# Crossbar DMA transposes and casting weight loads in an attention and MLP kernel

## The chip, the cores and the metric

The kernel runs on one core of one Trainium2 chip. The metric is the device time of one execution in microseconds (us). A profile is one execution recorded by the hardware profiler; its span, from the first to the last instruction, is about 2 us shorter than the timed run.

Engine names: PE is TensorE (matmuls and transposes), PEld its weight loads, DVE is VectorE, ACT is ScalarE, POOL is GpSimd, SP is SyncE, which only issues DMAs here. A name with q at the end (SPq) is that engine's sequencer or its DMA queue.

## The reference

Two parts in sequence: an attention with exponential feature maps, and a normalised two-layer MLP with a residual.

```python
# q, k, v: (8, 8, 576, 64); w_phi: (64, 128); w_ch1: (512, 2048); w_ch2: (2048, 512)
def phi(x):
    proj = x @ w_phi
    proj = proj - max(abs(proj), axis=-1)
    return concat([exp(proj), exp(-proj)], axis=-1)
q_p, k_p = phi(q), phi(k)
kv  = einsum('bhsf,bhsd->bhfd', k_p, v);   z = sum(k_p, axis=2)
num = einsum('bhsf,bhfd->bhsd', q_p, kv);  den = einsum('bhsf,bhf->bhs', q_p, z) + 1e-6
x   = heads_to_columns(num / den)                      # (8, 576, 512)
xn  = (x - mean(x)) / sqrt(var(x) + 1e-6) * g_ln
out = x + relu(xn @ w_ch1) @ w_ch2
```

## The kernel before

The batch is worked in four pairs of two. A pair has eight attention units, then a normalised x of nine tiles of 128 tokens, then the MLP on these. A list scheduler in the program fixes the order of the instructions on every engine beforehand: each operation is added with an estimate of its time, a rank, the keys that it reads and writes, and the engines that may do it. So all engines run in a fixed order, and an operation that waits holds up all that stand behind it on its engine. The MLP of one pair is interleaved with the attention of the next.

In the profile `qkT_ps` and `qkT` are transposed q and k, `pm` and `pt` their feature products, `kv` and `num` the attention products, `xc` the centred tokens, `xT` their transposes, `hT` the first MLP product (768 matmuls) and `ch` the second.

Every transpose is a TensorE matmul against an identity. It writes to PSUM, the memory of TensorE's results, and VectorE or ScalarE then copies (evicts) it to SBUF, where the operands of the next matmul lie:

```python
def a_trans(u, V):                       # q and k of one unit
    def products(i):
        qkb = qk_bufs[g % NBUF].bitcast(BF16)
        # ... PSUM tile qkT_ps ...
        for c in range(4):
            nc.tensor.transpose(
                u["qkT_ps"][:, (i * 4 + c) * P : (i * 4 + c + 1) * P],
                qkb[:, i, u["uu"], 4 * c * D + 1 : 4 * (c + 1) * D : 2], ident)
    def copy(e, i):
        # ...
        copy_on(e, u["qkT"][:, i * 512 : (i + 1) * 512], u["qkT_ps"][:, i * 512 : (i + 1) * 512])
    # ... i = 1 for k, 0 for q; the copies on DVE or ACT
```

```python
def center():                            # always on VectorE
    # ... r = t // NM, and the tile xc
    nc.vector.tensor_scalar(out=pr["xc", r][:, t % NM, :], in0=x[:, t, :],
                            scalar1=pr["mv"][:, t, 0:1], scalar2=None, op0=ALU.subtract)
# x_trans: 3 transposes of xc into a PSUM tile for each of 4 column blocks, then copies to xT
```

The weights come as fp32 into staging (the x buffers of later pairs), and are cast to bf16 by ScalarE or GpSimd; w1 is multiplied by g on the way:

```python
def load_w1(n, queue, rank):             # issued from SP
    dma(queue, rank, 1 << 20, stage(n), moe_w_ch1[...], w=[("stage", n % 2)])
def cast_w1(n, rank):
    # for each kc: w1_sb[...] = stage(n)[...] * gln_sb[:, kc]   on ACT or POOL
def cast_w2(n, rank):
    # for each block: w2_sb[...] = stage(n)[...]                on ACT or POOL
```

## Time and profile before

| | before |
|---|---|
| median of 2 runs | 419.39 us (418.72 to 420.06) |
| span of the profile | 417.9 us |
| TensorE busy | 371.7 us, 89% |
| first hT product | 66.7 us |

The first part of the page of the kernel before gives busy time, share of the span and number of instructions of each engine:

```profile
PE 371.7 (89%) x3575; PEld 229.1 (55%) x3632; DVE 274.7 (66%) x705; ACT 268.1 (64%) x569; POOL 171.7 (41%) x336
```

Averages hide that there are two stages. The windows view of the kernel before has, for each stretch: its length, busy us of each engine (with the number of instructions), the granted TensorE clock, the busy share of the 16 DMA engines and GB/s:

```profile
core 0: us, PE busy (x) PEld busy (x) DVE busy (x) ACT busy (x) POOL busy (x), PEclk, DMA share, GB/s
...
20.00:60.00 40.00, 26.29 (x339) 19.55 (x344) 32.17 (x93) 33.06 (x69) 37.06 (x68) 0.79 1.10 271
60.00:100.00 40.00, 30.59 (x316) 19.97 (x319) 31.42 (x85) 29.41 (x68) 23.68 (x47) 0.91 0.65 186
100.00:140.00 40.00, 39.20 (x411) 24.34 (x416) 27.21 (x67) 25.43 (x55) 14.86 (x32) 1.00 0.37 113
```

From 100 us on TensorE is full at full clock. From 20 to 60 us it is starved, at a clock of 0.79, while GpSimd is busy 37.1 of 40 us. The chain of waits of the kernel before (start, length, what) shows GpSimd as the engine that was waited for in that stretch:

```profile
52.04 1.55 POOL w L359
53.60 0.51 POOL x L718 x2
54.10 1.00 POOL vv L605
...
60.02 3.08 POOL w L359 x2
```

`w L359` is the cast and scaling of w1. What the transposes cost TensorE is read from the timeline of the kernel before (start, length, engine, line, operation), by the distance between starts, because the ends of pipelined matmuls overlap:

```profile
111.46 0.39 PE L513 MATMUL qkT_ps<-ident,qk 128*128 128x128 bf16 x4
111.69 0.81 PE L945 MATMUL ch_ps<-w,hT 128*128 128x512 bf16 x3
112.33 0.39 PE L513 MATMUL qkT_ps<-ident,qk 128*128 128x128 bf16 x4
112.56 0.81 PE L915 MATMUL hT_ps<-xT,w 128*128 128x384 bf16 x4
```

Four transposes hold TensorE for 0.22 to 0.23 us, 55 to 57 ns each. The mean durations in the next view are longer, about 220 to 240 ns, and must not be used as a cost. In the groups view of the kernel before (line, engine, operation, number; busy us and mean ns; idle time before, with releasers) these are the groups that the change touches:

```profile
L513 PE MATMUL qkT_ps<-ident,qk 128*128 128x128 bf16 x256 | 27.5, 241 | 6.0 <-DMA qk<-in_k_dram 5.0 <-DMA qk<-in_q_dram 0.7
L870 PE MATMUL xT_ps<-ident,xc 128*128 128x128 bf16 x144 | 14.3, 219 | 1.0 <-DVE xc L841 0.3 <-DVE hT L923 0.3 <-DVE numc L706 0.2
L359 POOL TENSOR_SCALAR w<-x,gln 128x512 bf16<-128x512 f32 x10 | 15.5, 1563 | 1.3 <-DMA x<-in_moe_w_ch_dram 1.3
L841 DVE TENSOR_SCALAR xc<-x,mv 128x512 bf16<-128x512 bf16 x36 | 14.1, 409 | 0.0
```

### The profile page before, as it was taken

What the parts mean: (1) busy time and instruction counts of PE and PEld (TensorE: products, weight loads), DVE (VectorE), ACT (ScalarE), POOL (GpSimd) and SP (SyncE); (2) the same over time, 40 slices, a digit from 0 to 9 for tenths busy, and PEclk for the clock granted to TensorE, in tenths of its full rate; (3) what the DMA queues carried; (4) which work ended last, traced back from release to release, by engine and by line L of the source; (5) the groups of instructions that cost most, each with busy time, mean ns of one, the idle gap of its engine ahead of it and who ended that gap; (6) DMA issues with size and microseconds to landing.
All of it is one profiled execution on the core that took longest, in us unless ns stands there. A gap on an engine that the chain in (4) does not pass through costs nothing.

```text
span 417.9 us, 9371 instructions
## 1 busy us (share of the span) xinstructions
PE 371.7 (89%) x3575; PEld 229.1 (55%) x3632; DVE 274.7 (66%) x705; ACT 268.1 (64%) x569; POOL 171.7 (41%) x336
## 2 busy tenths in 40 slices
PE   3657756888999899989999999889999999999995
PEld 2545534555556565656666655566565655555542
DVE  3768976987676779897567878966676778110111
ACT  4978884877585766876666757785667725533320
POOL 4799896553444453153243534344444420000000
PEclk9986797999999999999999999999999999999999
DMA  7999999742314641414242423300100001001003
GB/s 198 339 249 261 289 301 258 216 142 78 108 49 135 171 148 50 127 53 127 77 127 76 127 77 121 109 2 5 49 27 27 27 34 54 16 27 50 27 25 100
DMA packets 48956, 46.81 MB, mean 112 GB/s; under 512 B 15504, under 2 KB 40208, under 8 KB 48912
## 3 DMA queue, kind: packets, MB, share of 16 engines
q1 hardware_dynamic: 47680, 45.62, 37.2%
q10 hardware_dynamic: 1232, 0.59, 0.5%
q8 instruction: 28, 0.46, 0.5%
q14 instruction: 16, 0.13, 0.1%
HBM read 36.77 MB, written 9.44 MB: 111 GB/s over the span
## 4 chain that ended last, share of the span: by engine, by line
PE 69%; DVE 14%; POOL 5%; SPq 4%; ACT 3%; DMA 2%; issue 2%; DVEq 0%; ACTq 0%
PE ch_ps L945 27%; PE hT_ps L915 25%; SPq L275 4%; PE num L694 4%; DVE m L562 4%; PE kv L663 3%; DVE st L834 3%; PE pm L543 3%; PE qkT_ps L513 3%; DVE xc L841 2%; POOL vv L605 2%; PE pt L636 2%; POOL x L718 1%; DMA v<-in_v_dram 1%; DVE numc L700 1%
## 5 line engine op out<-in xcount | busy, mean ns | idle before, releaser
L915 PE MATMUL hT_ps<-xT,w 128*128 128x384 bf16 x768 | 151.9, 327 | 3.6 <-ACT hT L925 1.2
L945 PE MATMUL ch_ps<-w,hT 128*128 128x512 bf16 x536 | 143.8, 379 | 4.3 <-DVE qkT L266 1.6
L925 ACT ACTIVATE hT<-hT_ps 128x384 bf16<-128x384 f32 x140 | 68.1, 491 | 75.0 <-PE hT_ps L915 74.4
L718 POOL TENSOR_TENSOR x<-numc,rden 128x192 bf16<-128x192 f32 (+1 forms) x112 | 50.7, 462 | 120.4 <-DVE rden L712 107.3
L915 PEld LDWEIGHTS <-w 128*128 128x128 bf16 x768 | 71.0, 98 | 53.3 <-issue 4.5
L562 DVE TENSOR_REDUCE m<-pm 128x8 f32<-128x1024 f32 x64 | 76.5, 1209 | 8.1 <-PE pm L543 8.0
L945 PEld LDWEIGHTS <-hT 128*128 128x128 bf16 x576 | 50.9, 98 | 43.1 <-DVE qkT L266 2.1
L642 ACT ACTIVATE ea<-pt 128x1024 bf16<-128x1024 f32 x64 | 63.1, 1032 | 5.2 <-PE num L694 2.7
L591 ACT ACTIVATE EB<-pm 128x1024 bf16<-128x1024 f32 x64 | 63.4, 1023 | 0.6 <-DVE m L562 0.6
L952 DVE SCALAR_TENSOR_TENSOR o<-ch_ps,rstd,x 128x512 f32<-128x512 f32 x36 | 26.5, 743 | 50.6 <-PE ch_ps L945 50.2
L605 POOL TENSOR_TENSOR vv<-v,emk 128x512 bf16<-128x512 f32 x32 | 33.6, 1051 | 54.6 <-issue 29.1
L700 DVE TENSOR_TENSOR numc<-num,emq 128x195 f32<-128x195 f32 (+1 forms) x96 | 33.0, 347 | 29.1 <-PE num L694 21.3
L694 PEld LDWEIGHTS <-ea 128*128 128x128 bf16 x512 | 29.3, 102 | 15.3 <-issue 2.4
L923 DVE TENSOR_SCALAR hT<-hT_ps 128x384 bf16<-128x384 f32 x52 | 28.4, 546 | 12.4 <-PE hT_ps L915 12.0
L694 PE MATMUL num<-KV,ea 128*128 128x65 bf16 x512 | 33.6, 199 | 2.4 <-DVE qkT L266 0.8
L706 DVE TENSOR_TENSOR numc<-numc,num 128x195 f32<-128x195 f32 (+1 forms) x100 | 33.7, 344 | 1.4
L605 POOL TENSOR_TENSOR vv<-v,en 128x512 bf16<-128x512 f32 x32 | 33.4, 1044 | 0.6 <-DVE rden L712 0.3
L513 PE MATMUL qkT_ps<-ident,qk 128*128 128x128 bf16 x256 | 27.5, 241 | 6.0 <-DMA qk<-in_k_dram 5.0
L663 PEld LDWEIGHTS <-EB 128*128 128x128 bf16 x512 | 23.9, 103 | 11.9 <-issue 9.0
L663 PE MATMUL kv<-vv,EB 128*128 128x65 bf16 x512 | 28.2, 201 | 0.0
L513 PEld LDWEIGHTS <-qk 128*128 128x128 bf16 x256 | 20.1, 108 | 14.4 <-DMA qk<-in_k_dram 5.8
L834 DVE BATCH_NORM_STATS2 st<-x 128x6 f32<-128x512 bf16 x36 | 24.5, 680 | 2.7 <-POOL x L718 2.7
(64 smaller groups left out, 410.4 us busy)
## 6 DMA issues: line engine op xcount, KB each, us to landing
x<-in_moe_w_ch_dram SPq DMA_DIRECT2D x8, 1024.0 KB, 8.7
out_dram<-o SPq DMA_DIRECT2D x32, 256.0 KB, 2.3
qk<-in_k_dram SPq DMA_DIRECT2D x28, 256.0 KB, 3.6
v<-in_v_dram SPq DMA_DIRECT2D x28, 256.0 KB, 3.3
qk<-in_q_dram SPq DMA_DIRECT2D x26, 256.0 KB, 4.9
qk<-in_k_dram SPq DMA_DIRECT2D x2, 512.0 KB, 9.3
qk<-in_q_dram SPq DMA_DIRECT2D x2, 512.0 KB, 10.2
v<-in_v_dram SPq DMA_DIRECT2D x2, 512.0 KB, 9.1
```

Source lines behind the costliest of these rows:

```text
L513: nc.tensor.transpose(u["qkT_ps"][:, (i * 4 + c) * P : (i * 4 + c + 1) * P], qkb[:, i, u["uu"], 4 * c * D + 1 : 4 * (c + 1) * D : 2], ident,)
L562: nc.vector.reduce_max(out=u["m", i].rearrange("p (c e) -> p e c", e=2), in_=u["pm", i], axis=AX.X, apply_absolute_value=True,)
L591: nc.scalar.activation(u["EB"][:, t].rearrange("p c f -> p (c f)"), u["pm", 1].rearrange("p e c f -> p (e c f)"), AF.Exp, scale=(1.0, -1.0 ...
L605: nc.gpsimd.tensor_tensor(out=u["vv"][:, t, 0:MX, 0:D], in0=vb[:, uu, :].rearrange("p (c d) -> p c d", d=D), in1=bcast(e[:, 0:MX], 2, D), ...
L642: nc.scalar.activation(u["EA"][:, t, :], u["pt"], AF.Exp, scale=(1.0, -1.0)[t])
L663: nc.tensor.matmul(ps[:, t, c // 4, :], EB[:, t, (c % 2) * 4 + c // 2, :], vv[:, t, c, :], start=False, stop=(t == 0 and c == MX - 1), ski ...
L694: nc.tensor.matmul(ps[:, t, i, :], lhsT, rhs, start=(j == 0), stop=(j == len(terms) - 1))
L700: nc.vector.tensor_tensor(out=st["numc"][:, 0:nch], in0=st["ps"][:, 1], in1=bcast(em_of(), 2, D1), op=ALU.mult,)
L718: nc.gpsimd.tensor_tensor(out=dst, in0=st["numc"][:, i : i + cnt, 0:D], in1=bcast(st["rden"][:, i : i + cnt], 2, D), op=ALU.mult,)
L915: nc.tensor.matmul(st["ps"], w1_sb[:, kc, jj * P : (jj + 1) * P], pr["xT", r][:, kc, :], start=(kc == 0), stop=(kc == KC - 1),)
L925: nc.scalar.activation(h_sb, st["ps"], AF.Relu)
L945: nc.tensor.matmul(ch[t], hT[r, jj][:, rt * P : (rt + 1) * P], w2_sb[:, jj, :], start=(jj == 0), stop=(jj == JC - 1),)
```

## The change

The intent is to take transposes from TensorE and casts from GpSimd. (1) From the second pair on, q and k of a unit are cast to bf16 in one instruction, and one DMA that transposes on its way (`dma_start_transpose`, called a crossbar transpose here) writes `qkT`; `xc` goes to `xT` in the same way. (2) The weights are cast by the DMA that loads them, issued by GpSimd and held back until a `vv` product on GpSimd; g is then multiplied into w1 in place by VectorE or GpSimd. (3) Centring may go to VectorE or GpSimd. Around this the change makes the xT evictions wider and the x keys finer, gives `qkT` three buffers in place of two and x three in place of four, and reorders priorities. Its core:

```diff
+        if u["pair"]:
+            def cast(e):
+                u["qkb"] = att.tile([P, 2, MX * D], BF16, tag="qkb", name="qkb")
+                copy_on(e, u["qkb"], qk_bufs[g % NBUF][:, :, u["uu"], :])
+            def turn():
+                u["qkT"] = att.tile([P, 1024], BF16, tag="qkT", name="qkT", bufs=NQ)
+                nc.sync.dma_start_transpose(
+                    out=u["qkT"].rearrange("p (c n) -> p c n", n=P),
+                    in_=u["qkb"].rearrange("p i f -> p (i f)"))
+            add_any({"POOL": 1.1, "ACT": 0.95, "DVE": 0.6}, V, cast, ...)
+            add("SP", 0.7, V, turn, ...)
+            add("DMA", 1.0, V, None, ...)
+            return
 ...
+            add_any({"DVE": 0.25, "POOL": 0.75}, V, center, ...)        # was DVE alone
 ...
+        if pr["pair"]:
+            for i in range(n):
+                def turn(i=i):
 ...
+                    nc.sync.dma_start_transpose(
+                        out=pr["xT", r][:, :, i * P : (i + 1) * P], in_=pr["xc", r][:, i, :])
 ...
-    def load_w1(n, queue, rank):        # fp32 into stage(n), then cast_w1 on ACT or POOL
+    def load_w1(n, rank, after):
+        dma("POOL", rank, 1200000, w1_sb[:, :, n * WC : (n + 1) * WC], moe_w_ch1[...],
+            r=after, w=[("w1", n, kc) for kc in range(KC)])
+    def scale_w1(n, rank):
+        ...
+                w = w1_sb[:, kc, n * WC : (n + 1) * WC]
+                ENG[e].tensor_scalar_mul(out=w, in0=w, scalar1=gln_sb[:, kc : kc + 1])
+            add_any({"DVE": 0.22, "POOL": 0.62}, rank, emit, ...)
 ...
+                after = [("vv", 0, n % 2)]
```

## The prediction

> **What bounds the kernel now.** Two stages. From 100 to 413 us TensorE is the bound: the windows view has it busy 303.4 of 313 us at clock 1.00, and the waits view gives it no wait above 1.6 us there. Before that it is starved: in 0 to 66.7 us it is busy 40.4 us at a mean clock of 0.83, with DMA share 1.03, ACT 50.9 and GpSimd 55.6. The first hT product stands at 66.7 us, when all 144 kv products of pair 0 are issued. From 28 to 66 us the chain of waits runs again and again through GpSimd (vv, x, and three w1 casts of 1.56 us between 52 and 63 us); TensorE's largest wait there is kv on GpSimd's vv, 8.5 us.
>
> **What the change removes.** In TensorE order, 192 of 256 qkT transposes and 108 of 144 xT transposes. Timeline, steady stage: four transposes hold TensorE 0.22 us start to start, 55 ns each. The Trainium skill ("TensorE: Matmul & The Clock Gate", "Wait — 56ns, not 53.3ns?") says 55.6; the trace agrees. So 300 x 55.6 ns = 16.7 us off the bounding engine, nearly all on the path. Their evictions go too (qkT halves 0.42 us DVE, 0.59 us ACT), and the staged weight casts: 15.5+4.9 us GpSimd, 8.7 us ACT.
>
> **What it adds.** 24 q/k casts, mostly on ACT (about 1 us, estimated from the 1.03 us ACT passes over 128x1024), and 51 crossbar transposes on the SP queue, 9.8 MB, against a DMA share of 0.23. In the start-up: five w1 scalings on GpSimd (1.56 us, if like the casts), eleven on DVE (0.41 us, like centring), eight GpSimd-issued weight DMAs[...]. All 27 later centrings move to GpSimd, probably 1.5 us each against 0.41 on DVE. "VectorE: DVE Perf Modes" (The three transpose paths) gives 1309 ns for one 128x128 crossbar transpose; if eight serialised, 10.5 us would fill a unit's slot (about 11 us). I expect them spread over engines and 3 to 5 us to landing, hidden by three qkT buffers.
>
> **Start-up.** The new TensorE order puts the first hT at kv 108, not 144; 64 hT (10.4 us) stand before kv 144. With GpSimd freed of casts I expect the first hT near 57 us and the steady stage about 10 us earlier.
>
> **Give-back.** At each of the three pair boundaries stats, GpSimd centring and crossbar are a longer chain than before; before, TensorE lost 3.1 us at 260-280. I allow 4-5 us in all.
>
> **Sum.** 419.4 - 16.7 - 10 + 4 = about 397 us. I say 396, 8 in 10 from 382 to 409. Faster by over 2%: 0.93; within 2%: 0.06; slower: 0.01.
>
> **What would show it.** 64 qkT and 36 centred transposes left on TensorE; first hT at 55-60 us; no TensorE wait on qkT's crossbar DMA above 2 us; short TensorE holes at the pair boundaries; a higher DMA share; GpSimd busy about 40 us up by centring, 20 down by casts.
>
> **What would make it wrong.** Crossbar transposes slow or serialised (over 8 us landing), so that TensorE waits for qkT or xT; SP's in-order queue holding loads or stores behind a transpose that waits for its cast; casting DMAs taking several us of GpSimd each, or taking start-up bandwidth so that q/k/v land late; GpSimd centring opening holes of 5 us or more per pair. Or, downward, a much shorter start-up (385 or less).

## More of the kernel before

Part 3 of the page of the kernel before gives packets, megabytes and the share of the 16 DMA engines' time for each queue:

```profile
q1 hardware_dynamic: 47680, 45.62, 37.2%
```

## The result

The changed kernel took 398.84 us (398.57 to 399.10, two runs), against 419.39 before: a ratio of 0.951, with an interval of 0.9439 to 0.9581. A ratio here is the mean time of one kernel's fast runs over that of the other's of the same rounds, so not quite the ratio of the medians. The later sets have their own runs of the kernel before, with medians of 419.66 to 420.44 us. Differences in us from the changed kernel are taken below between medians, against 398.84.

The first part of the page of the changed kernel:

```profile
PE 358.1 (90%) x3332; PEld 211.0 (53%) x3332; DVE 264.9 (67%) x652; ACT 253.2 (64%) x522; POOL 212.4 (54%) x362
```

The groups of the changed kernel that answer to those above:

```profile
L523 PE MATMUL qkT_ps<-ident,qk 128*128 128x128 bf16 x64 | 8.5, 283 | 6.1 <-DMA qk<-in_k_dram 5.2 <-DMA qk<-in_q_dram 0.9
L903 PE MATMUL xT_ps<-ident,xc 128*128 128x128 bf16 x36 | 3.8, 249 | 6.2 <-DVE numc L716 5.1 <-POOL xc L853 0.9
L363 DVE TENSOR_SCALAR w<-w,gln 128x512 bf16<-128x512 bf16 x11 | 8.9, 855 | 0.0
L363 POOL TENSOR_SCALAR w<-w,gln 128x512 bf16<-128x512 bf16 x5 | 7.8, 1569 | 0.0
L853 POOL TENSOR_SCALAR xc<-x,mv 128x512 bf16<-128x512 bf16 x27 | 42.1, 1572 | 8.7 <-DVE mv L848 5.8
L265 ACT CAST qkb<-qk 128x1024 bf16<-128x1024 f32 x16 | 16.6, 1044 | 7.0 <-DMA qkT<-qkb 6.6 <-POOL x L728 0.3
```

The counts are as predicted: 64 and 36 transposes are left, 27 centrings went to GpSimd at 1.57 us. The windows of the changed kernel, in the same stretches:

```profile
20.00:60.00 40.00, 26.42 (x331) 18.52 (x331) 36.54 (x93) 32.20 (x67) 34.85 (x61) 0.74 1.08 236
60.00:100.00 40.00, 33.92 (x345) 21.01 (x345) 28.50 (x80) 27.00 (x62) 25.40 (x46) 1.00 0.76 159
100.00:140.00 40.00, 39.16 (x454) 23.96 (x451) 34.44 (x85) 33.97 (x66) 26.42 (x52) 1.00 0.75 197
```

From 20 to 60 us TensorE is no busier than before (26.4 against 26.3 us). GpSimd was relieved of only 2.2 us, and VectorE took 4.4 us more. The chain of waits of the changed kernel at that place now runs through VectorE:

```profile
56.35 1.21 DVE m L572
...
58.99 0.76 DVE w L363 x2
59.75 0.16 issue
59.91 0.69 DVE w L363
```

In the steady stage no wait of TensorE for the crossbar is long. The waits view of the changed kernel, TensorE alone, from 100 to 395 us (total, times, longest) begins:

```profile
PE kv L668 <- ACT eax L451: 1.4, 1, 1.4
PE hT_ps L953 <- DMA xT<-xc: 1.2, 1, 1.2
PE ch_ps L985 <- ACT eax L451: 0.7, 1, 0.7
```

The DMA view of the changed kernel gives the queues, and for the transposes their number and the median us from issue to landing:

```profile
q1 hardware_dynamic: 83488, 47.07, 47.3%
q0 software_dynamic: 4224, 4.19, 6.7%
...
w<-in_moe_w_ch_dram POOLq DMA_DIRECT2D x8, 512.0 KB, 9.6
...
xT<-xc SPq DMA_TRANSPOSE x27, 2.5
qkT<-qkb SPq DMA_TRANSPOSE x24, 3.4
```

### Where the 21 us came from

I split each span into work and lost time. Work is an estimate: the number of TensorE instructions of each kind times about their distance from start to start at full clock in the timelines (hT 162.5 ns, ch and pt 215.7, a transpose 55.6, kv 31.5, num 31, pm 29, the few px and wide kv products 56 to 110). The profile of the kernel before lacks 57 matmul records (3575 of 3632, 40 of them ch and 17 pt); they are counted by their weight loads. Lost is the rest of the span: idle time, half clock, and the tail after the last matmul.

| | work | lost up to 100 us | lost 100 to 280 us | lost after 280 us | span |
|---|---|---|---|---|---|
| before | 346.6 | 51.8 | 12.6 | 6.9 | 417.9 |
| changed | 329.9 | 47.3 | 12.4 | 6.9 | 396.5 |
| difference | -16.7 | -4.5 | -0.2 | 0.0 | -21.4 |

The work falls by 300 x 55.6 ns by the way it is counted; what the table adds is that lost time did not grow in return. The start-up gave 4.5 us and not 10, and nothing was given back later. Each row is one profile: up to 100 us the runs below, e4 apart, lost 44.9 to 50.3 us by the same count, so the 4.5 is uncertain by some 3 us. This is an accounting; whether the parts cause it is for the experiments.

### The profile page after: what moved, and what is told of

It reads as the page before. It is cut to its first block, busy times and chain, and to the rows that moved or that the text cites. A ratio compares the mean times of both kernels' runs of the same rounds, so it can differ in the third digit from the quotient of the medians.

```text
span 396.5 us, 8895 instructions
## 1 busy us (share of the span) xinstructions
PE 358.1 (90%) x3332; PEld 211.0 (53%) x3332; DVE 264.9 (67%) x652; ACT 253.2 (64%) x522; POOL 212.4 (54%) x362
## 3 DMA queue, kind: packets, MB, share of 16 engines
q1 hardware_dynamic: 83488, 47.07, 47.3%
q0 software_dynamic: 4224, 4.19, 6.7%
## 4 chain that ended last, share of the span: by engine, by line
PE 66%; DVE 17%; DMA 8%; issue 3%; ACT 2%; POOL 2%; SPq 0%; DVEq 0%; POOLq 0%; ACTq 0%
PE ch_ps L985 27%; PE hT_ps L953 25%; DVE m L572 5%; PE num L704 3%; PE kv L673 3%; PE pm L553 3%; DMA qkT<-qkb 2%; PE pt L646 2%; DMA kx<-in_k_dram 2%; DVE numc L710 2%; DVE st L847 2%; DVE numc L716 2%; DVE w L363 1%; DMA qk<-in_k_dram 1%; DMA v<-in_v_dram 1%
## 5 line engine op out<-in xcount | busy, mean ns | idle before, releaser
L953 PE MATMUL hT_ps<-xT,w 128*128 128x384 bf16 x768 | 149.5, 326 | 4.3 <-DVE numc L716 1.3
L985 PE MATMUL ch_ps<-w,hT 128*128 128x512 bf16 x576 | 148.4, 379 | 1.7 <-ACT eax L451 0.7
L963 ACT ACTIVATE hT<-hT_ps 128x384 bf16<-128x384 f32 x132 | 64.0, 490 | 73.8 <-PE hT_ps L953 73.5
L985 PEld LDWEIGHTS <-hT 128*128 128x128 bf16 x576 | 52.6, 98 | 47.2 <-DVE numc L716 0.8
L652 ACT ACTIVATE ea<-pt 128x1024 bf16<-128x1024 f32 x64 | 62.2, 1026 | 5.6 <-PE pt L646 5.3
L992 DVE SCALAR_TENSOR_TENSOR o<-ch_ps,rstd,x 128x512 f32<-128x512 f32 x36 | 26.5, 743 | 56.5 <-PE ch_ps L985 43.9
L853 POOL TENSOR_SCALAR xc<-x,mv 128x512 bf16<-128x512 bf16 x27 | 42.1, 1572 | 8.7 <-DVE mv L848 5.8
L710 DVE TENSOR_TENSOR numc<-num,emq 128x195 f32<-128x195 f32 (+1 forms) x96 | 32.6, 345 | 18.1 <-PE num L704 12.2
L961 DVE TENSOR_SCALAR hT<-hT_ps 128x384 bf16<-128x384 f32 x60 | 32.4, 544 | 13.7 <-PE hT_ps L953 13.2
L704 PEld LDWEIGHTS <-ea 128*128 128x128 bf16 x512 | 28.2, 100 | 18.9 <-issue 3.7
L704 PE MATMUL num<-KV,ea 128*128 128x65 bf16 x512 | 32.5, 197 | 3.9 <-DVE numc L716 1.8
L553 PEld LDWEIGHTS <-qkT 64*128 64x128 bf16 x512 | 16.0, 100 | 13.1 <-issue 11.0
```

Source lines behind the costliest of these rows:

```text
L652: nc.scalar.activation(u["EA"][:, t, :], u["pt"], AF.Exp, scale=(1.0, -1.0)[t])
L704: nc.tensor.matmul(ps[:, t, i, :], lhsT, rhs, start=(j == 0), stop=(j == len(terms) - 1))
L853: ENG[e].tensor_scalar(out=pr["xc", r][:, i, :], in0=x[:, t, :], scalar1=pr["mv"][:, t, 0:1], scalar2=None, op0=ALU.subtract,)
L953: nc.tensor.matmul(st["ps"][:, 0:cols], w1_sb[:, kc, jj * P : (jj + 1) * P], pr["xT", r][:, kc, 0:cols], start=(kc == 0), stop=(kc == KC - 1),
L963: nc.scalar.activation(h_sb[:, 0:cols], st["ps"][:, 0:cols], AF.Relu)
L985: nc.tensor.matmul(ch[t], hT[r, jj][:, rt * P : (rt + 1) * P], w2_sb[:, jj, :], start=(jj == 0), stop=(jj == JC - 1),)
```

## The experiments

The theory A says: the time saved is that of the removed TensorE work, 16.7 us, on an engine that bounds the steady stage. Its rivals: the start-up path with the new weights gives a large share; the scaling of w1 in place holds the start-up back (D); GpSimd's slow centring gives time back at the pair boundaries (H); the crossbar is free, or is near a limit, by the time that it holds its source buffer or by the load on crossbar and DMA engines (I and J). Each kernel is the changed kernel with one edit. Two of them, e4 and e12, give wrong results on purpose; all others were correct.

### e3_no_crossbar: all transposes back on TensorE, new weight path kept

```diff
-        if u["pair"]:          # in a_trans
+        if False:
-        if pr["pair"]:         # in x_trans
+        if False:
```

> The changed kernel with q, k and the centred tokens transposed on TensorE in all pairs again; the new weight path is kept. Theory A (the gain is 16.5 us of removed TensorE work plus about 5 us of start-up): 398.8 + 16.5 = about 415 us, 413 to 417, and a first hT product still near 52 us. Rival B (the start-up is worth the 10 us that was predicted, and the crossbar nets only about 10): 408 to 410 us.

Measured: 417.77 us (415.93 to 418.42), ratio 0.9938 [0.9904, 0.9972]. All of the change but the crossbar gives 2.6 us. Adding the crossbar to it gives 18.9 us between medians; the ratios (0.9938 to 0.951) say 18. In the accounting e3's work is 346.6 us and the crossbar takes 16.7 from it.

### e8_old_weights: crossbar kept, old weight path

The fp32 staging, the casts on ScalarE and GpSimd and the loads by SP of the kernel before were put back, staged in x buffers that the changed kernel has, with the dependencies that this needs, and without the new leads for the start-up.

```diff
-    dma("POOL", rank, 1200000, w1_sb[...], moe_w_ch1[...], r=after, ...)
+    dma(queue, rank, 1 << 20, stage(n), moe_w_ch1[...], w=[("stage", n % 2)])
-    scale_w1 in place on DVE or POOL
+    cast_w1, cast_w2 from stage(n) on ACT or POOL
```

> The changed kernel with the old weight path: float32 weights loaded on the SP queue into staging areas, cast and scaled on ACT and GpSimd; the crossbar transposes are kept. Theory A: before minus the removed TensorE work, 419.4 - 16.5 = about 403 us, 401 to 405. Rival B (the start-up is worth 10 us): 408 to 410 us.

Measured: 398.09 us (397.55 to 398.85), ratio 0.9478 [0.945, 0.9505], the same as the changed kernel. So the new weight path is not needed for the gain. Its profile has 47.9 us lost up to 100 us, against 47.3 with the new path and 51.8 before; e3 has 47.4. A start-up gain of about 4 us is thus there with either weight path, and with or without the crossbar (e1, below, is an exception: 50.3). What e3 and e8 share against the kernel before is the rest of the change (wider xT evictions, finer x keys, the buffers, other priorities). Which of these gives the 4 us was not tested.

### e1_qk_on_pe and e2_xt_on_pe: one of the two crossbar uses alone

```diff
-        if u["pair"]:          # e1, in a_trans: 192 q and k transposes back
+        if False:
```
```diff
-        if pr["pair"]:         # e2, in x_trans: 108 xc transposes back
+        if False:
```

> The changed kernel with q and k alone back on TensorE in all pairs, with their evictions and without casts and crossbar; centred tokens stay on the crossbar. Theory A (each removed transpose was worth its 55.6 ns on TensorE): 398.8 + 10.7 = 409.5 us, 408 to 411. Theory F (half of the TensorE time put back falls into holes, as the 4.8 us of the work-back run suggests, and nothing else of this part matters): 403 to 405 us.

> The changed kernel with the centred tokens alone back on TensorE, 108 transposes and their evictions; q and k stay on the crossbar. Theory A: 398.8 + 6.0 = about 405 us, 404 to 406.5. Theory G (the crossbar's longer chain costs some us at the pair boundaries, so that undoing it gives part back): 400 to 403 us.

Measured: e1 407.49 us (407.12 to 409.07), ratio 0.9706 [0.9672, 0.974], so 8.7 us over the changed kernel where 192 x 55.6 ns = 10.7; e2 404.47 us (404.37 to 407.12), ratio 0.9647 [0.9601, 0.9694], 5.6 us over it, where 108 x 55.6 ns = 6.0. The two parts carry the gain nearly in proportion to the TensorE work that each removes. The evictions on VectorE and ScalarE come back in the same proportion, so this alone does not separate the two. The accounting does: in the profiles of e1, e2 and e3 the work is 10.7, 6.0 and 16.7 us above the changed kernel's, and all lost time together is 66.0, 66.8 and 67.6 us against 66.6. From 100 to 280 us they lost 8.4, 11.9 and 11.7 us, no more than its 12.4. The evictions that came back opened no more holes in TensorE; what came back in the time is TensorE's own work. That supports A.

### e5_pe_work_back: TensorE work put back, its result not read

The crossbar stays; TensorE does the 192 q and k transposes as well, into a PSUM tile that nobody reads.

```diff
+            def again():
+                ps = ps_B.tile([P, 1024], BF16, tag="B", name="again_ps")
+                for c in range(8):
+                    nc.tensor.transpose(ps[:, c * P : (c + 1) * P],
+                        u["qkb"].rearrange("p i f -> p (i f)")[:, c * P : (c + 1) * P], ident)
+            add("PE", mm(8, 128), V, again, r=[("qkb", n % 2)], w=[("again", n)],
+                acquire=("B", 1), release=[("B", 1)])
```

> The changed kernel, crossbar transposes kept, and the 192 q/k transposes of pairs 1 to 3 also done on TensorE into a PSUM tile that nobody reads (no eviction). Theory A (TensorE time is what was saved): 192 x 55.6 ns = 10.7 us slower, 408 to 411 us. Rival C (the saving is the evictions that ACT and DVE no longer do): under 401 us.

Measured: 403.63 us (402.49 to 404.69), ratio 0.9604 [0.9567, 0.9641]: 4.8 us over the changed kernel, of the 10.7 put back. Both theories missed. In the accounting the work rises by 10.7 us and the lost time falls from 66.6 to 61.8 (2.4 us of that before 100 us, 2.7 from 100 to 280): the sum is as if half of the added work lay in time that was lost anyway. So "TensorE is full" is true only nearly. But the run is not clean. The extra transposes read the q/k tile, and the scheduler moved the casts after them: these start 24.8 us ahead of use in the mean and not 33.8, and their waits for a crossbar transpose (11.5 us in the changed kernel) are gone, with 4.2 us of waits for the extra transposes in their place. Whether the work slid into holes, or the new order won part of it back, was not separated. In e1 the same 10.7 us cost 8.7.

### e4_no_gscale: the scaling of w1 dropped (wrong on purpose)

```diff
-                    scale_w1(i_, V)
+                    pass
```

> The changed kernel without the scaling of w1 by g; the result is wrong on purpose. Theory D (the start-up gained little because the scalings fill DVE and GpSimd from 28 to 60 us, 8.9 and 7.8 us busy): 3 to 5 us faster than the changed kernel, 394 to 396 us, with lost TensorE time mainly saved between 40 and 70 us. Rival E (the start-up is held by the loads: DMA share above 1 from 20 to 80 us): within 1 us of 398.8.

Measured: 399.31 us (398.04 to 403.09), ratio 0.9521 [0.9467, 0.9574]: no gain. Yet the start-up was faster. The windows of e4:

```profile
20.00:60.00 40.00, 30.01 (x377) 20.92 (x375) 33.54 (x98) 34.67 (x72) 35.18 (x70) 0.79 1.13 247
60.00:100.00 40.00, 35.17 (x347) 21.02 (x346) 26.70 (x76) 24.85 (x55) 22.89 (x39) 1.00 0.88 166
100.00:140.00 40.00, 35.80 (x423) 21.69 (x421) 34.05 (x78) 33.55 (x65) 24.86 (x49) 1.00 0.79 186
```

From 20 to 60 us VectorE is 3.0 us less busy than in the changed kernel and TensorE 3.6 us more; the last kv product of pair 0 came at 62.5 us and not at 67.6. By 100 us e4 had lost 42.1 us, 5.2 less. But from 100 to 280 us it lost 18.1 and not 12.4. So the scaling does seem to hold the start-up back (one profile, but below all the others up to 100 us), and D as a cause of the total time falls: the 5 us are taken again. The waits of e4, TensorE alone, from 100 to 200 us:

```profile
PE ch_ps L985 <- DVE hT L961: 1.9, 1, 1.9
PE pt L646 <- DVE m L572: 1.6, 1, 1.6
PE hT_ps L953 <- DVE hT L961: 0.9, 1, 0.9
```

These are waits for VectorE, two for evictions of `hT` and one for the maximum `m`; in the same stretch of the changed kernel the longest is 0.5 us. VectorE and ScalarE are both about 85% busy from 100 to 140 us in either kernel (before: 68% and 64%). That VectorE and ScalarE now set the pace just after the start-up fits these lines, but no run showed it by itself.

### e12_small_weights: the weight loads at a quarter of their bytes (wrong on purpose)

```diff
-            "POOL", rank, 1200000, w1_sb[:, :, n * WC : (n + 1) * WC], moe_w_ch1[...]
+            "POOL", rank, 1200000, w1_sb[:, 0:1, n * WC : (n + 1) * WC], moe_w_ch1[0:P, ...]
+    nc.vector.memset(w1_sb, 0.0)        # w2 in the same way
```

> The changed kernel with weight loads of a quarter of the bytes (the rest of the weights is zero; the result is wrong on purpose): 6.3 MB fewer read in the first 80 us. Theory E (the start-up is held by the loads): the last kv product of pair 0 before 62 us instead of 67.5, and 4 us or more off the total. Rival K (the start-up is a chain of ACT, DVE and GpSimd work, and what it gains early is lost again in pair 1, as without scaling): kv within 3 us of 67.5 or the total within 2 us of 398.8.

Measured: 400.7 us (400.23 to 401.04), ratio 0.9548 [0.9534, 0.9561]: no gain, rather 2 us lost, with two large fills added to VectorE at the start. Up to 100 us it lost 48.9 us, and the last kv product of pair 0 came at 68.9. Less load traffic showed no gain in the start-up; but the two fills hold VectorE for 3.5 us each between 2 and 10 us, so a gain of a few us could be hidden behind them.

### e6_center_dve: centring on VectorE alone

```diff
-            add_any({"DVE": 0.25, "POOL": 0.75}, V, center, ...)
+            add_any({"DVE": 0.35}, V, center, ...)
```

> The changed kernel with all 36 centrings on DVE, about 0.35 us each, in place of 27 on GpSimd at 1.57 us. Theory G (the predicted give-back at the pair boundaries, through GpSimd's slow centring, is real): 394 to 397 us. Rival H (the boundaries are covered by other TensorE work): within 1.5 us of 398.8, or slower because DVE is 85% busy from 100 to 140 us.

Measured: 398.13 us (397.26 to 399.03), ratio 0.9476 [0.9445, 0.9508]. It cannot be told from the changed kernel. Taking 42 us from GpSimd moved nothing measurable, so the give-back of 4 us, named in the prediction, was not there to be recovered. The windows of two pair boundaries, one profile each, show gains and losses that net out. First the changed kernel, then e6:

```profile
140.00:160.00 20.00, 20.00 (x161) 10.76 (x159) 16.40 (x40) 11.52 (x27) 14.26 (x19) 1.00 0.78 166
240.00:280.00 40.00, 36.51 (x344) 21.69 (x344) 27.39 (x70) 26.82 (x60) 23.61 (x35) 1.00 0.42 95
```
```profile
140.00:160.00 20.00, 17.93 (x139) 9.43 (x138) 13.74 (x37) 12.24 (x26) 8.48 (x17) 0.91 0.69 157
240.00:280.00 40.00, 39.26 (x374) 23.34 (x372) 31.64 (x86) 29.28 (x67) 18.86 (x37) 1.00 0.46 100
```

At 240 to 280 us TensorE gains 2.8 us, at 140 to 160 it loses 2.1 and its clock falls to 0.91. There e6 loses 4.1 us, and a q/k cast on ScalarE stands idle for 3.9 us at that place, for something that the profile does not name.

### e9_crossbar_twice and e10_crossbar_beside: what a crossbar transpose costs

e9 transposes each q/k tile twice, the second time into a tile that nobody reads. e10 does the second transpose from the weights instead, so that the q/k tile is not held longer.

```diff
+                twin = att.tile([P, 1024], BF16, tag="twin", name="twin", bufs=1)
+                nc.sync.dma_start_transpose(
+                    out=twin.rearrange("p (c n) -> p c n", n=P),
+                    in_=u["qkb"].rearrange("p i f -> p (i f)"))     # e10: in_=w1_sb[:, 0, 0:1024]
```

> The changed kernel with each q/k crossbar transpose issued twice, the second into a tile that nobody reads; 6.3 MB more through the crossbar. Theory A (the crossbar has room; landing 3.4 us, hidden): within 1.5 us of 398.8. Rival I (DMA, at a share of 0.75 from 100 to 180 us, and the in-order SP queue are near their limit): 404 us or more.

> As the run with each q/k crossbar transpose doubled, but the second one reads the resting weights, so that no cast waits for its source to come free. Same bytes, same packets, same SP issues. Theory I (crossbar, DMA engines or SP queue near their limit): again 410 us or more. Theory J (the doubled run lost its 17 us because casts, in order on ACT and GpSimd, waited 38 us for a qkb buffer that the second transpose still read): 402 us or less.

Measured: e9 415.92 us (413.58 to 418.35), ratio 0.99 [0.9843, 0.9957], 17 us over the changed kernel; e10 407.51 us (404.26 to 409.32), ratio 0.9702 [0.9663, 0.9741], 8.7 us over it. The groups of e9 show where it waits:

```profile
L265 ACT CAST qkb<-qk 128x1024 bf16<-128x1024 f32 x16 | 16.6, 1045 | 26.4 <-DMA twin<-qkb 26.4
L267 POOL CAST qkb<-qk 128x1024 bf16<-128x1024 f32 x4 | 4.1, 1037 | 9.8 <-DMA twin<-qkb 7.3 <-issue 2.5
```

and the same groups of e10:

```profile
L265 ACT CAST qkb<-qk 128x1024 bf16<-128x1024 f32 x16 | 16.6, 1044 | 16.5 <-DMA qkT<-qkb 13.7 <-issue 2.1 <-POOL x L732 0.7
L267 POOL CAST qkb<-qk 128x1024 bf16<-128x1024 f32 x4 | 4.1, 1036 | 8.0 <-DMA qkT<-qkb 6.8 <-issue 1.1
```

A cast waits until the transpose two units earlier has read its tile. With the twin on the same tile the wait is 38 us in all (with 4.4 us on VectorE), with the twin beside it 22, in the changed kernel 11.5. In e9 TensorE waits for no q/k transpose from 100 to 395 us; its longest wait there, 3.9 us at 192 us, is for an `hT` eviction on ScalarE that stood right behind a cast, and this cast had waited 6.2 us for a twin. That is how a wait of the casts reaches TensorE. So about half of e9's cost goes with the longer hold on the source. The other half stays when the source is free, but e10 does not tell its cause: it doubles the traffic and also SyncE's issues, and each transpose held SyncE for about 1.25 us in the median (an ordinary load 0.49), with 7.1 us more of waits there for the single twin tile. The crossbar path is not free: it is hidden in the changed kernel, but there is no room for a second one of the same size.

### e11_qkb3: three q/k source tiles and not two

```diff
-                u["qkb"] = att.tile([P, 2, MX * D], BF16, tag="qkb", name="qkb")
+                u["qkb"] = att.tile([P, 2, MX * D], BF16, tag="qkb", name="qkb", bufs=3)
-    keys ("qkb", n % 2)
+    keys ("qkb", n % 3)
```

> The changed kernel with three qkb buffers instead of two. Theory J (part of what is left is casts that wait for a crossbar transpose to let go of its buffer: 11.5 us of such waits on ACT, GpSimd and DVE in the changed kernel): these waits go, and 1 to 3 us faster, 396 to 398 us. Rival: within 0.5 us of the changed kernel, because ACT and DVE have time to spare there.

Measured: 399.89 us (398.84 to 402.0, five runs), ratio 0.953 [0.9506, 0.9553]: no gain, and the casts still wait 13.7 us in all for a qkT transpose. A miss. By the trace, the casts start 33.8 us ahead of their unit's first feature product in the mean in the changed kernel, and 42.0 us in e11: the third tile only lets the scheduler issue the casts earlier, where they wait again. Every `qkT` of the changed kernel landed at least 8.5 us before that product. With so much lead neither the waits nor the landing of 3.4 us decide when TensorE gets its `qkT`.

### e13_cast_pool: e6 with all q/k casts on GpSimd

```diff
-            add_any({"POOL": 1.1, "ACT": 0.95, "DVE": 0.6}, V, cast, ...)
+            add_any({"POOL": 1.05}, V, cast, ...)
```

> The changed kernel (398.8 us) with the centring on VectorE alone, as in the earlier run of that edit (398.1), and all 24 q/k casts on GpSimd (about 1.04 us each) instead of 16 on ScalarE, 4 on VectorE and 4 on GpSimd. This takes 16.7 us of casts from ScalarE and 3.8 us from VectorE, and puts 20.8 us on a GpSimd that lost 42.1 us of centring. If the steady stage is held up by casts that stand in the in-order queue of ScalarE or VectorE and wait there for a load or for a qkb buffer (11.5 us of such waits in the changed kernel, and the stall of 4.1 us at 140 to 150 us with the centring on VectorE), the waits move to GpSimd, where nothing urgent stands behind them, and the time falls to 392 to 396 us. If TensorE is the bound and those waits are in slack, it stays within 1.5 us of 398.1. If GpSimd's slower reaction delays the crossbar, the TensorE stream waits for qkT by DMA and the time rises above 400.

Measured: 401.34 us (399.85 to 402.67, five runs), ratio 0.954 [0.9522, 0.9558]. It is slower than e6 (the intervals do not meet), so the hope of 392 to 396 falls. The group of the casts in e13:

```profile
L267 POOL CAST qkb<-qk 128x1024 bf16<-128x1024 f32 x24 | 24.8, 1038 | 17.4 <-DMA qkT<-qkb 15.9 <-issue 1.5
```

The waits did move to GpSimd, and grew from 13 us in e6 (2.4, 8.8 and 1.8 on the three engines) to 15.9. What stands behind them is not idle work: `vv` and `x` come from GpSimd too. The time is above 400 us, as in the third branch of the expectation, but its reason, TensorE waiting for a late qkT, did not come: the largest waits from 100 to 160 us are for VectorE's `m` (1.9 us in two waits) and `numc` (1.3). From 100 to 280 us e13 lost 15.5 us, against 12.4 in e6, in many small waits, and what starts them stays open. No version tried beats the changed kernel by more than the noise.

## Why the prediction was right

The time, 398.84 us, is inside 382 to 409 and 2.8 us above the 396 predicted. The sum was "419.4 - 16.7 - 10 + 4 = about 397 us". Term by term:

| term of the sum | predicted | measured, and by what |
|---|---|---|
| transposes off TensorE | -16.7 | -16.7 of work by count, with lost time no greater; -18 to -19 from e3 to the changed kernel; 8.7 + 5.6 = 14.3 in two parts (e1, e2) |
| steady stage earlier | -10 | -4.5 of lost time up to 100 us; -2.6 for all but the crossbar (e3); none for the new weight path beside the crossbar (e8) |
| give-back at pair boundaries | +4 | -0.2 of lost time from 100 to 280 us; no gain from centring on VectorE (e6) |

**The bound and the main term held.** TensorE bounds the steady stage, and 300 x 55.6 ns came off its path: put back with all that belongs to it (e1, e2, e3), this work came back in the time and lost time hardly moved. The Trainium skill ("TensorE: Matmul & The Clock Gate", "Wait — 56ns, not 53.3ns?") gives 55.6 ns between starts; the trace has 55 to 57. e5 sets a limit to the reasoning: the same kind of work, put back without users, cost 4.8 us of its 10.7.

**The step that failed is the start-up:** "With GpSimd freed of casts I expect the first hT near 57 us and the steady stage about 10 us earlier." The first hT came even earlier, at 51.7 us. The inference from it failed. The prediction has 64 hT products (10.4 us) before kv 144, the last kv product of pair 0. In the trace of the changed kernel 36 stand there, 36 x 162.5 ns = 5.9 us, and that kv product came 2 us later than before, at 67.6 us against 65.6. So the early hT products filled holes of an attention that was itself no faster, and the 4.5 us fit their number. That this is the whole of it is not shown: e8 has 8 hT products there, its last kv product at 64.4 us, and lost no more up to 100 us (47.9). GpSimd was not freed either: 34.9 of 40 us from 20 to 60 us against 37.1, and 40.7 us busier over the span.

One term of that step was mis-sized in a way that could have been seen. I took "eleven on DVE (0.41 us, like centring)". They took 0.855 us in the mean, 0.34 to 1.75, and the chain at 59 us runs through them. The slowest, of 1.755 us, spanned one of GpSimd's own scalings (1.552 us) from start to end. In e6, 28 of 36 centrings, a VectorE instruction of the same kind and shape, ran with nothing at the same time on GpSimd, and took 0.32 to 0.36 us; the slow ones, up to 0.91, all overlapped GpSimd instructions. The Trainium skill ("SBUF — State Buffer", "SBUF: two separate sides") says that VectorE, in some of its modes, and GpSimd take one shared port pair as "an exclusive lock, not a bandwidth split", for a whole instruction. The trace fits that, although it does not record the lock. Read so, work moved from a busy GpSimd to VectorE still waited for GpSimd.

**The other error had the opposite sign.** The give-back of 4 us did not come; TensorE had interleaved MLP work to do meanwhile, though no run showed that to be the reason. The boundary at 240 to 280 us does lose time (36.5 of 40 us busy), but it lost as much before (36.3). The two errors, about 5 and 4 us, nearly cancelled. That was luck, and it is why a sum with one term twice too large hit the total so closely.

**Why a faster start-up is worth little.** e4 is the evidence: 5 us gained up to 100 us, all lost again by 280. That VectorE and ScalarE set the pace there is the likely cause, not a shown one.

**The crossbar was as fast as I hoped and not free.** Landing took 3.4 us (predicted 3 to 5), the casts run 34 us ahead of use, and TensorE waited at most 1.2 us for a transpose. The risk named as "crossbar transposes slow or serialised" did not come; e9 and e10 show that a second transpose of every q/k tile would have cost 9 to 17 us.

## What to carry to other kernels

Count work on the bounding engine by the distance between starts; here three runs that put it back with its users paid for nearly all of it, and one that put it back alone paid for half. An experiment that puts work back also changes the order of a scheduled program, so look at what else moved. An earlier first product is no earlier stage: count how much work stands ahead of the old bottleneck, and ask whether a gain there survives until the end. Moving work from GpSimd to VectorE while GpSimd stays busy can pay twice (0.855 us in the mean here for a planned 0.41), so take VectorE's time from instructions that ran beside a busy GpSimd.

## What the Trainium skill lacked or had wrong

- "Advanced Engine Details and Errata", X-Bar Transpose (TRN2), says that "TRN2 transpose DMAs are as fast as regular DMAs" and expects 350-400 GB/s. In the changed kernel's packet records the 256-byte packets, of which the transposes add 38,400, take 24 ns of a DMA engine each, so 16 x 256 B / 24 ns = 171 GB/s over 16 engines, an estimate from the mean. The 2,048-byte packets of its ordinary DMAs take 93 ns (352 GB/s), those of 1,024 bytes 54 ns (303 GB/s). So the expected bandwidth was not reached. But the 12,288 packets of 256 bytes in the kernel before, all of ordinary DMAs, took 24 ns too: packet for packet the transposes were as fast, as the page says. What it lacks there is that these transposes moved in packets of 256 bytes.
- "VectorE: DVE Perf Modes", The three transpose paths, gives 1309 ns for one 128x128 block by crossbar and 390 ns by TensorE. It does not say that several blocks in one DMA overlap: eight landed in 3.4 us in the median, four in 2.5. In a full TensorE stream a transpose held the engine 55 to 57 ns, so its 390 is not the price that counts there.
- "DMA: Bandwidth & Descriptors", SWDGE vs HWDGE vs iDMA, says that a cast during a DMA must come from GpSimd; here it does. It gives no price for the cast. Here the casting load wrote 1,024-byte packets at 104 ns each, 26.5 us of all 16 engines for 4.19 MB of bf16; reading the same weights as fp32 in the kernel before took 4,096 packets of 2,048 bytes at 101 ns, 25.7 us. The cast saved no DMA engine time, and each issue held GpSimd 0.84 us.
- "SBUF — State Buffer", SBUF: two separate sides, has the lock between VectorE and GpSimd right as far as the runs show, without a number for one-input bf16 work: 0.34 us became up to 1.75 us for a VectorE scaling of 128x512.
- "GPSIMD Engine Reference", 3.1 Elementwise — side-by-side cycle accounting, has a best case of 769 ns for 512 elements and about 2.6 cycles an element for two inputs. The two-input product `vv` of 128x512 took 1.05 us, near the 1.11 us that 512 x 2.6 cycles at the page's 1.2 GHz would give (an estimate). The one-input scaling and centring of the same shape in bf16 took 1.57 us, longer than with two inputs, which the page does not have.
